# A fused attention and MLP kernel: one score product issued a step ahead, and a copy out of PSUM issued behind an exponential

## The chip, the cores and the metric

The kernel runs on one core of one Trainium2 chip. The metric is the time of one execution on the device in microseconds (us). Before the change it is 755.63 us, the median of three runs (755.60 to 755.68).

## What is computed

`x` has 2048 tokens of 512 channels. It is normalized, goes through an attention with 32 heads of 16 channels in which each token sees the 256 tokens up to itself, and through an MLP with 1792 hidden channels; the result is `x + s * silu(MLP)`.

```python
def _A_ref(x, wqkv, wo):          # H = 32, Dh = 16, W = 256
    q, k, v = qkv[0], qkv[1], qkv[2]
    scores = jnp.einsum("bhqd,bhkd->bhqk", q, k) * (Dh ** -0.5)
    mask = (idx[:, None] - idx[None, :] >= 0) & (idx[:, None] - idx[None, :] < W)
    p = _softmax(jnp.where(mask[None, None], scores, -1e9), axis=-1)
    o = jnp.einsum("bhqk,bhkd->bhqd", p, v)
    return o @ wo
...
def _B_ref(x, w1, b1, w2, b2):
    h = _gelu(_layernorm(x) @ w1 + b1)
    return h @ w2 + b2
...
xn = _layernorm(x)
s = _A_ref(xn, A_wqkv, A_wo)
g = _silu(_B_ref(xn, B_w1, B_b1, B_w2, B_b2))
return x + s * g
```

## The kernel before

Every engine runs its instructions in the order of the program text (`Ordered`); waits between engines are put in by the framework from the tiles that two instructions share. All matrix products are in single precision, split into a high and a low part where they are large.

**The attention loop.** The 32 heads are worked on four at a time (`n` = 0 to 7), in 16 blocks of 128 tokens, so there are 128 steps `t` = 16n + block. A first pass of 16 steps with negative `t` prepares the first heads. In step `t` TensorE (PE) issues, in this order:

1. `prob_block(..., 1)`: two products of keys and queries for two of the four heads into the PSUM tile `stb`. ScalarE (ACT) takes the exponential of it into a tile `pt` in SBUF, and GpSimd (POOL) zeroes what the mask excludes. There is one `stb`, so the next products into it wait for this exponential.
2. `max_block`, for the block `m = t + 12`, twelve steps ahead: four products into `xy` (the two newer key blocks), then, from the third block of a head on, four products into `zo[:, :, 0:256]` (the oldest key block, of which a triangle counts). VectorE (DVE) then copies that triangle from `zo` over the masked triangle of `xy` (`copy_predicated`), and reduces `xy` to its negated row maximum (`tensor_reduce`), which is later subtracted in the softmax. For the first two blocks of a head there is no oldest block, and the masked copy reads a constant instead of `zo`.
3. `fill_in(t, 0)`: a share of other matrix work, the "fills".
4. `prob_block(..., 0)`: the products and the exponential for the other two heads, through the same `stb`.
5. `fill_in(t, 1)`: more fills.
6. `pv_step`, for block `t - 1`: twelve products of probabilities and values (four for the first block of a head, eight for the second), in tiles of 128 rows by 17 columns, into `otb`. This is not a tile of its own but `zo[:, 1, 256:384]`. ACT then copies it into `oraw` in SBUF.

In what follows the exponential of 1 is called the **first** and that of 4 the **second** exponential of a step, and the stretch of a step that begins with each its first and second **half**. In the last twelve steps there is no block left for `max_block`, and the first products of a step go into `xy`.

**The fills.** The fills of the steps from 3 on are made by `tandem`: two jobs (`pair_qk`: projections of queries and keys for later heads; `pair_v`: of the values; `pair_h`: hidden products of the MLP) run through the two PSUM banks `fb[0]` and `fb[1]` at once. A unit is a pair of products of 64 rows each, one into each bank; two jobs of `pair_qk` are 24 units. When both jobs end, ACT copies bank 0 and DVE bank 1 (`closing`), and the next two jobs begin. `room(t, k)` says how many units half `k` of a step may take before others are preferred: mostly three in the first half and one in the second.

**After the loop** come the rest of the MLP, the output projection and the final sums, from about 435 us on, almost all of it a dense stream of products. The change does not touch that part.

Of the kernel before, what the change touches and what calls it, by code (L numbers as in the profile page):

```python
# [18 lines left out]
P = 128  # L19
NCH = S // 512  # L20
NKB = S // P
KT = D // P
# [27 lines left out]
def mixer_kernel(ctx, tc, x, wqk, wv, wo, w1, b1, w2, b2, out):  # L50


    nc = SimpleNamespace(**{name: Ordered(tc, name) for name in ("tensor", "vector", "scalar", "gpsimd", "sync")})
# [117 lines left out]
    slots = []  # L171
# [8 lines left out]
    oT_d = dram.tile([4, 8, 32, S], F32, name="oT_d")  # L180
# [8 lines left out]
    xy = psum.tile([P, 2, 512], F32, name="xy")  # L189
    zo = psum.tile([P, 2, 512], F32, name="zo")  # L190
    otb = zo[:, 1, 256:384]
    psf = attn.enter_context(tc.tile_pool(name="psf", bufs=1, space=PSUM))
    fb = [psf.tile([P, 512], F32, name=f"fb{i}") for i in range(2)]
# [103 lines left out]
    fills = {}  # L297
    closing = {}
# [145 lines left out]
    def tandem(t0, t1, one, two, mid=None, back=None):  # L444

        n = one[0]
        lo, hi = slice(0, 64), slice(64, P)
        mid = mid or max(1, (t0 + t1 + 1) // 2)  # L450
        late = t1 >= 16 * NQ - LEAD

        def room(t, k):

            m = t % 16
            if k:
                return {1: 3, 2: 2, 14: 2, 15: 2}.get(m, 1)
            return 2 if t == t0 else {4: 4, 15: 2}.get(m, 3)

        def places(slots, last):  # L460

            halves = [(t, k) for t in slots for k in (0, 1)] + [(t1, 0)] * last
            units = dict.fromkeys(halves, 0)
            for _ in range(n - last * n // 12):
                h = min(units, key=lambda h: (units[h] >= room(*h) * n // 12, units[h]))
                units[h] += 1
            if last:
                units[t1, 1] = n // 12
            return [h for h in units for _ in range(units[h])]

        def places_late(slots, last):

            last = min(n // 4, n // (len(slots) + 1)) if last else 0
            cuts = [(n - last) * k // len(slots) for k in range(len(slots) + 1)]
            out = []
            for t, a, b in zip(slots, cuts, cuts[1:]):
                ahead = min(b - a, max(n // 4, (b - a + 1) // 2))
                out += [(t, 0)] * ahead + [(t, 1)] * (b - a - ahead)
            return out + [(t1, 0)] * last

        deal = places_late if late else places
        first, second = deal(range(t0, mid), False), deal(range(back or mid, t1), True)
        for phase, where in enumerate((first, second)):
            for i in range(n):
                flags = dict(start=(phase == 0 and i == 0), stop=(phase == 1 and i == n - 1), skip_group_check=True)
                def unit(i=i, phase=phase, flags=flags):
                    (two if phase == 0 else one)[1](fb[1 - phase], i, hi, **flags)
                    (one if phase == 0 else two)[1](fb[phase], i, lo, **flags)
                fills.setdefault(where[i], []).append((unit, ()))
        closing[t1] = (one[2], (fb[0], t1, nc.scalar.copy)), (two[2], (fb[1], t1, nc.vector.tensor_copy))  # L490
        if late:
            fills[t1, 0].extend(closing.pop(t1))

    def spread(jobs, places):

        out, left = {}, list(places)
        for j, (ops, finish) in enumerate(jobs):
            n = round(len(left) / (len(jobs) - j))
            mine, left = left[:n], left[n:]
            for k, (_, mm, i) in enumerate(ops):  # L500
                out.setdefault(mine[k * n // len(ops)], []).append((mm, (i,)))
            out[mine[-1]].append((finish, ()))
        return out
# [1 line left out]

    mts = {}

    def max_block(n, qb):

        slot = slots[n % 2]  # L510
        if qb % 4 == 0:
            mts[n, qb // 4] = small.tile([P, 2, 2, 4], F32, tag="mt", name=f"mt_{n}_{qb}")
        lo = max(qb - 1, 0)
        off = 128 * (lo + 1 - qb)

        def scores(p, a, first):
            r = slice(64 * a, 64 * a + 64)
            out, keys = ((zo[:, a, P * p: P * (p + 1)], slice(P * (qb - 2), P * (qb - 1))) if first else
                         (xy[:, a, 256 * p + off: 256 * (p + 1)], slice(P * lo, P * (qb + 1))))
            nc.tensor.matmul(out, slot[r, 0, p, P * qb: P * (qb + 1)], slot[r, 1, p, keys], start=True, stop=True)  # L520

        for p, a, first in ((0, 1, False), (0, 0, False), (1, 1, False), (1, 0, False),
                            (0, 1, True), (0, 0, True), (1, 1, True), (1, 0, True)):
            if qb >= 2 or not first:
                scores(p, a, first)
        four = xy.rearrange("q a (p k) -> q a p k", p=2)
        nc.vector.copy_predicated(four[:, :, :, 128:256], mask,
                                  neg if qb < 2 else zo[:, :, 0:256].rearrange("q a (p k) -> q a p k", p=2))
        nc.vector.tensor_reduce(out=mts[n, qb // 4][:, :, :, qb % 4],
                                in_=four[:, :, :, off:256],  # L530
                                axis=AX.X, op=ALU.max, negate=True)
# [41 lines left out]
        pts[(n, kb, p)] = pt  # L573


    outs = {}

    def pv_step(n, qb):

        lo = max(qb - 2, 0)  # L580
        for kb in range(lo, qb + 1):
            for j in range(4):
                nc.tensor.matmul(otb[32 * j: 32 * j + DH + 1], vt[:, kb, (4 * n + j) % 16],
                                 pts[n, kb, j // 2][:, j % 2, P * (qb - kb): P * (qb - kb + 1)],
                                 start=(kb == lo), stop=(kb == qb),
                                 skip_group_check=True, tile_position=(0, 32 * j))
        if qb % 4 == 0:
            outs[0] = sgp.tile([P, 512], F32, tag="or", name=f"oraw_{n}_{qb}", bufs=2)
        nc.scalar.copy(outs[0][:, P * (qb % 4): P * (qb % 4 + 1)], otb)
        if qb % 4 == 3:  # L590
            (at if n or qb > 7 else behind)(16 * n + qb + 2, nc.sync.dma_start, oT_d[n // 2, n % 2::2, :, P * (qb - 3): P * (qb + 1)], outs[0])


    mlp = {}
# [151 lines left out]
        fills.setdefault(place, []).extend(todo)  # L746
    soon = {}
    tandem(3, 8, pair_qk(1, 2), pair_qk(1, 3))
    for n, spans in enumerate((((9, 14, 12), (15, 19, 18)), ((20, 24, 22), (25, 30, 28)), ((31, 35, 34), (36, 40, 38)),
                               ((41, 46, 44), (47, 51, 50)), ((74, 79, 77), (80, 84, 83)), ((85, 90, 88), (93, 98, 97))), 2):  # L750
        for c, span in zip((0, 2), spans):
            tandem(*span[:2], pair_qk(n, c), pair_qk(n, c + 1), *span[2:])
    for i, span in enumerate(((52, 56, 54), (57, 62, 60), (63, 67, 66), (68, 73, 71))):
        tandem(*span[:2], pair_v(2 * i), pair_v(2 * i + 1), *span[2:])
    for f, *span in ((6, 99, 104, 102), (8, 105, 110, 108), (10, 111, 115, 114), (12, 116, 121, 118, 119), (2, 122, 127, 124, 125)):
# [59 lines left out]
    def fill_in(t, half):  # L815
        now[:] = t, half
        run(delayed.pop((t, half), ()))
        for fn, args in fills.get((t, half), ()):
            fn(*args)

    end = 16 * NQ
    for t in range(-16, end + 1):
        m = t + LEAD
        if t == -5:
            open_slot(1)
            for k in range(4):
                at(-4 + k, clear_part, k)
        if 0 <= t < end:
            if t == 0:
                early.close()  # L830
                stb.append(attn.enter_context(tc.tile_pool(name="ps_s2", bufs=1, space=PSUM)).tile(
                    [P, 2, 512], F32, name="stb"))
            prob_block(t // 16, t % 16, 1)
        if t >= 0 and m < end:
            max_block(m // 16, m % 16)
        fill_in(t, 0)
        for fn, args in plan.get(t, []):
            fn(*args)
        if m == 1:
            max_block(0, 1)  # L840
        if 0 <= t < end:
            prob_block(t // 16, t % 16, 0)
        fill_in(t, 1)
        if m == 0 or 1 <= m < LEAD - 1:
            max_block(0, m + (m > 0))
        for fn, args in closing.get(t, ()):
            fn(*args)
        if t >= 1:
            pv_step((t - 1) // 16, (t - 1) % 16)
        run(lns.get(t, ()))  # L850
        done = m if t >= 0 else m + 1 if 0 < m < LEAD - 1 else 0
        if done < end and done % 4 == 3:
            max_rows(done // 16, done % 16 // 4, t)
        for fn, args in ends.get(t, []):
            fn(*args)
    for k in sorted(delayed):
        run(delayed[k])
    for fn, args in plan[end + 1]:
# [440 lines left out]
```

## Time and profile before

| | us |
|---|---|
| time, median of three runs | 755.63 |
| the profiled execution's own time | 756.44 |
| its span, first to last instruction | 754.6 |
| first exponential of step 0 | 64.79 |
| first exponential of step 112 | 391.97 |
| last first exponential (step 127) | 429.87 |

In a view of the timeline each row has a start and a length in us, the engine, the operation and what it writes and reads (`out<-in`); `x4` at the end is four instructions in one row, and brackets hold the idle time of that engine before the row and what ended it. PEld is the weight load of TensorE, which runs ahead of the products. All rows carry line L42, since a helper records every operation; they are told apart by their tiles. `zo<-qk` are the oldest-block products, `zo<-pt,vt` those of probabilities and values, `fb<-...` the fills.

### The profile page before, as it was taken

How to read it: one execution, taken by the hardware profiler on the slowest of the kernel's cores; microseconds unless marked ns; L12 is line 12 of the kernel's file. 1: busy time of each engine (PE TensorE's matmuls, PEld its weight loads, DVE VectorE, ACT ScalarE, POOL GpSimd, SP SyncE). 2: the span in 40 equal slices, each digit the busy share in tenths (PEclk: the TensorE clock that was granted, in tenths of full speed). 3: DMA queues.
4: the chain of work that ended last, by engine and by line, in shares of the span. 5: the costliest groups of instructions: out<-in, count | busy, mean ns of one | idle time of the engine just before them, and what ended most of it. 6: DMA issues, size and time to landing. Idle time of an engine off the chain costs nothing.

```text
span 754.6 us, 18785 instructions
## 1 busy us (share of the span) xinstructions
PE 742.7 (98%) x7412; PEld 581.8 (77%) x7412; DVE 502.6 (67%) x770; ACT 438.5 (58%) x745; POOL 313.4 (42%) x658
## 2 busy tenths in 40 slices
PE   8999999999999999999999999999999999999997
PEld 7886776777778887676676788888888888888886
DVE  7876676776767767787872547853666765676373
ACT  7747767767667676787877845444554643442001
POOL 7623767777566565877876700030102000001102
PEclk9999999999999999999999999999999999999999
DMA  8623355645347763546725383542112232244531
GB/s 285 192 62 83 74 146 135 172 114 123 90 105 217 256 212 98 147 108 183 202 77 158 91 296 103 167 158 66 57 42 97 85 111 71 69 158 136 172 93 56
DMA packets 56951, 99.40 MB, mean 132 GB/s; under 512 B 11104, under 2 KB 11360, under 8 KB 56864
## 3 DMA queue, kind: packets, MB, share of 16 engines
q1 hardware_dynamic: 56864, 98.21, 44.4%
q8 instruction: 58, 0.95, 0.5%
q14 instruction: 29, 0.24, 0.1%
HBM read 51.39 MB, written 29.62 MB: 107 GB/s over the span
## 4 chain that ended last, share of the span: by engine, by line
PE 88%; DVE 4%; ACT 2%; DMA 2%; POOL 2%; issue 1%; SPq 0%; DVEq 0%; ACTq 0%; POOLq 0%
PE acc L42 20%; PE fb L42 17%; PE zo L42 13%; PE p L42 9%; PE stb L42 8%; PE s L42 6%; PE h L42 6%; PE xy L42 5%; PE pv L42 3%; POOL pt L42 1%; ACT pt L42 1%; DVE mt L42 1%; DVE xnT L42 1%; DVE xy L42 1%; DMA oT_d<-oraw 1%
## 5 line engine op out<-in xcount | busy, mean ns | idle before, releaser
L42 POOL TENSOR_SCALAR_AFFINE_SELECT pt<-pt 128x256 f32<-128x256 f32 x480 | 188.2, 417 | 121.8 <-ACT pt L42 118.0
L42 ACT ACTIVATE pt<-stb 128x768 f32<-128x768 f32 (+1 forms) x244 | 188.4, 772 | 59.9 <-PE stb L42 50.9
L42 DVE TENSOR_REDUCE mt<-xy 128x4 f32<-128x1024 f32 (+1 forms) x128 | 152.6, 1192 | 4.4
L42 DVE COPY_PREDICATED xy<-upper,zo 128x512 f32<-128x512 int32 x112 | 77.9, 696 | 87.6 <-PE zo L42 84.4
L42 PE MATMUL acc<-w,gh 128*128 128x512 f32 x432 | 133.5, 390 | 0.0
L42 PE MATMUL fb<-xnT,wqb 64*128 64x512 f32 (+1 forms) x684 | 116.3, 405 | 0.3 <-DVE xnT L42 0.2
L42 POOL TENSOR_TENSOR xo<-xo,gated 128x512 f32<-128x512 f32 x15 | 20.2, 1348 | 216.9 <-DVE gated L42 212.6
L42 PE MATMUL zo<-pt,vt 128*17 128x128 f32 x2880 | 103.8, 275 | 0.3 <-POOL pt L42 0.3
L42 PE MATMUL stb<-qk 64*128 64x384 f32 (+1 forms) x488 | 97.7, 396 | 2.5 <-ACT pt L42 0.8
L42 PEld LDWEIGHTS zo<-pt,vt 128*17 128x17 f32 x2880 | 67.6, 97 | 37.6 <-DVE xy L42 19.8
L42 PEld LDWEIGHTS acc<-w,gh 128*128 128x128 f32 x432 | 80.8, 188 | 16.6
L42 PE MATMUL acc<-w,gl 128*128 128x512 f32 x216 | 84.4, 391 | 0.0
L42 PEld LDWEIGHTS stb<-qk 64*128 64x128 f32 x488 | 45.7, 183 | 48.3 <-ACT pt L42 37.3
L42 PEld LDWEIGHTS fb<-xnT,wqb 64*128 64x128 f32 (+1 forms) x684 | 63.9, 187 | 7.0 <-issue 0.6
L42 PE MATMUL xy<-qk 64*128 64x256 f32 (+2 forms) x536 | 61.3, 302 | 1.4 <-DVE mt L42 1.0
L42 ACT COPY oraw<-zo 128x128 f32<-128x128 f32 x128 | 34.3, 268 | 37.4 <-PE zo L42 27.1
L42 PEld LDWEIGHTS xy<-qk 64*128 64x128 f32 x536 | 43.1, 185 | 11.2 <-DVE mt L42 4.5
L42 PEld LDWEIGHTS acc<-w,gl 128*128 128x128 f32 x216 | 40.6, 188 | 8.9 <-DVE gl L42 0.7
L42 ACT ACTIVATE gated<-acc 128x512 f32<-128x512 f32 x16 | 8.7, 595 | 65.2 <-DVE acc L42 65.2
L42 PE MATMUL s<-wos,ohl 128*128 128x512 f32 (+1 forms) x204 | 44.7, 378 | 0.0
L42 PEld LDWEIGHTS s<-wos,ohl 128*128 128x128 f32 x204 | 36.7, 188 | 6.9
L42 ACT COPY p<-p 128x512 f32<-128x512 f32 x21 | 12.3, 585 | 49.8 <-PE p L42 42.3
(198 smaller groups left out, 1196.5 us busy)
## 6 DMA issues: line engine op xcount, KB each, us to landing
qk<-sh SPq DMA_DIRECT2D x128, 128.0 KB
qk<-pjr SPq DMA_DIRECT2D x64, 128.0 KB
oT_d<-oraw SPq DMA_DIRECT2D x32, 256.0 KB
w_d<-in_w_dram SPq DMA_DIRECT2D x14, 512.0 KB
x<-in_x_dram SPq DMA_DIRECT2D x16, 256.0 KB
or<-oT_d SPq DMA_DIRECT2D x16, 256.0 KB
w<-rden_d SPq DMA_DIRECT2D x16, 256.0 KB
xo<-in_x_dram SPq DMA_DIRECT2D x16, 256.0 KB
```

The costliest lines, as they stand in the source:

```text
L42: r = issue(*args, **kwargs)
```

## The change

**Oldest-block products ahead.** `first_scores` holds the four products into `zo` that `max_block` had. They are now issued in the step before: behind `fill_in(t, 1)` and ahead of `pv_step`, for block `m + 1`. Blocks without an oldest block are left out, and three early ones keep their old place.

**The copy of the values.** `pv_step` no longer issues ACT's copy of `otb`. It leaves a function in the list `copies`, which is called in the next step, behind the first exponential and ahead of `max_block`.

**The fills.** `room` now gives four units to the first half and mostly none to the second. The eight window pairs of heads 2 to 5 (steps 9 to 51) go through the new `staggered`: the job in bank 1 starts four units behind that in bank 0 and ends four units into the next pair; both banks are copied by DVE, one step apart. The first four units at step 9 and the last four at step 51 are single products.

```diff
@@ room of tandem, and how halves are dealt
             m = t % 16
             if k:
-                return {1: 3, 2: 2, 14: 2, 15: 2}.get(m, 1)
-            return 2 if t == t0 else {4: 4, 15: 2}.get(m, 3)
+                return {1: 2, 2: 1, 3: 1, 4: 1}.get(m, 0)
+            return 3 if t == t0 else {5: 3, 15: 3}.get(m, 4)
...
+    AHEAD = 4
+    def staggered(windows):
...
+        for w, (t0, t1, mid, one, two) in enumerate(windows):
+            head = [(t0, 0)] * AHEAD
+            laid.append((head + deal(range(t0 + 1, mid), n - AHEAD, None, mid - 1), deal(range(mid, t1), n, t1)))
...
+            for i in range(n):
+                if i >= AHEAD:
+                    unit(first[i], two[1], 1, i - AHEAD, hi, i == AHEAD, False)
+                elif w:
+                    unit(first[i], windows[w - 1][4][1], 1, n - AHEAD + i, hi, False, i == AHEAD - 1)
+                unit(first[i], one[1], 0, i, lo, i == 0, False)
...
+            closing[t1] += ((one[2], (fb[0], t1, nc.vector.tensor_copy)),)
...
+            closing[t1 + 1] += ((two[2], (fb[1], t1, nc.vector.tensor_copy)),)
...
+    def first_scores(n, qb):
+        slot = slots[n % 2]
+        keys = slice(P * (qb - 2), P * (qb - 1))
+        for p in range(2):
+            for a in (1, 0):
+                r = slice(64 * a, 64 * a + 64)
+                nc.tensor.matmul(zo[:, a, P * p: P * (p + 1)], slot[r, 0, p, P * qb: P * (qb + 1)],
+                                 slot[r, 1, p, keys], start=True, stop=True)
...
+        if qb >= 2 and not ahead:
+            first_scores(n, qb)
         four = xy.rearrange("q a (p k) -> q a p k", p=2)
         nc.vector.copy_predicated(four[:, :, :, 128:256], mask,
                                   neg if qb < 2 else zo[:, :, 0:256].rearrange("q a (p k) -> q a p k", p=2))
...
-        nc.scalar.copy(outs[0][:, P * (qb % 4): P * (qb % 4 + 1)], otb)
+        out = outs[0]
+        def copy_out():
+            nc.scalar.copy(out[:, P * (qb % 4): P * (qb % 4 + 1)], otb)
+        copies.append(copy_out)
...
             prob_block(t // 16, t % 16, 1)
+        while copies:
+            copies.pop()()
         if t >= 0 and m < end:
-            max_block(m // 16, m % 16)
+            max_block(m // 16, m % 16, m in early_first)
...
         fill_in(t, 1)
+        if t >= 0 and m + 1 < end and (m + 1) % 16 >= 2 and ((m + 1) % 4 or m >= 32):
+            first_scores((m + 1) // 16, (m + 1) % 16)
+            early_first.add(m + 1)
```

**ACT, steps 42 to 44.** `pt_10`, `pt_11` and `pt_12` are the exponentials of these steps, `_1` the first and `_0` the second; `oraw<-zo` is the copy of the values. In brackets stand the engines on whose counts of finished instructions the row waits. Before:

```order
L42 ACTIVATE pt_10_0_2960<-stb 128x768 [waits PE_49]
L42 COPY oraw_8_2934<-zo 128x128 [waits DVE_49,PE_49]
L42 ACTIVATE pt_11_1_2982<-stb 128x768 [waits PE_49,Activation_49,Pool_49]
L42 ACTIVATE pt_11_0_3004<-stb 128x768 [waits PE_49]
L42 COPY oraw_8_2934<-zo 128x128 [waits DVE_49,PE_49]
L42 ACTIVATE pt_12_1_3029<-stb 128x768 [waits PE_49,Activation_49,Pool_49]
```

and now:

```order
L42 ACTIVATE pt_10_0_2966<-stb 128x768 [waits PE_49]
L42 ACTIVATE pt_11_1_2989<-stb 128x768 [waits PE_49,Activation_49,Pool_49]
L42 COPY oraw_8_2934<-zo 128x128 [waits DVE_49]
L42 ACTIVATE pt_11_0_3010<-stb 128x768 [waits PE_49]
L42 ACTIVATE pt_12_1_3036<-stb 128x768 [waits PE_49,Activation_49,Pool_49]
```

The copy moved from between the second exponential of one step and the first of the next to behind that first one.

**PE, second half of step 43.** `stb` are the products for the second exponential, `zo<-qk` the oldest-block products, `zo<-pt` those of probabilities and values. Before:

```order
L42 MATMUL stb<-qk_92 128x384 [waits Activation_49]
L42 MATMUL stb<-qk_92 128x384
L42 MATMUL fb_108<-xnT,wqb_2804 128x512
L42 MATMUL fb_109<-xnT,wqb_2804 128x512
L42 MATMUL zo<-pt_9_0_2912,vt 17x128 [waits DVE_49]
L42 MATMUL zo<-pt_9_0_2912,vt 17x128
L42 MATMUL zo<-pt_9_1_2889,vt 17x128 x2
L42 MATMUL zo<-pt_10_0_2960,vt 17x128 x2
L42 MATMUL zo<-pt_10_1_2938,vt 17x128 x2
L42 MATMUL zo<-pt_11_0_3004,vt 17x128 [waits Pool_49]
```

and now:

```order
L42 MATMUL stb<-qk_92 128x384 [waits Activation_49]
L42 MATMUL stb<-qk_92 128x384
L42 MATMUL zo<-qk_722 128x128 [waits DVE_49]
L42 MATMUL zo<-qk_722 128x128 x3
L42 MATMUL zo<-pt_9_0_2909,vt 17x128 x2
L42 MATMUL zo<-pt_9_1_2885,vt 17x128 x2
L42 MATMUL zo<-pt_10_0_2966,vt 17x128 x2
L42 MATMUL zo<-pt_10_1_2937,vt 17x128 x2
L42 MATMUL zo<-pt_11_0_3010,vt 17x128 [waits Pool_49]
```

The unit of fills went to the first half, the oldest-block products came in its place, and the wait on DVE now stands ahead of them.

**DVE, steps 67 to 69, now.** `COPY_PREDICATED` is the masked copy of `max_block`, reading `zo` in the first row and the constant `negc` in the fourth (the first block of a head). Both kinds of row read alike before the change:

```order
L42 COPY_PREDICATED xy<-upper,zo 128x4x128 [waits DVE_49,PE_49,Activation_49]
L42 TENSOR_REDUCE mt_12_4109<-xy 128x4 [waits DVE_49]
L42 COPY vt<-fb_109 128x32x16 [waits PE_49]
L42 COPY_PREDICATED xy<-upper,negc 128x4x128 [waits DVE_49,PE_49]
L42 TENSOR_REDUCE mt_0_4342<-xy 128x4 [waits DVE_49]
L42 STREAM_TRANSPOSE mT_3_4333<-mh_3_4330 128x32 [waits DMAHW1_49,Pool_49]
```

DVE's order of these rows did not move. A masked copy that reads `zo` waits for ACT, one that reads the constant does not. In the built program the ACT count that it waits for is, before and now, the one that the latest copy of the values reaches. That copy stood ahead of the first exponential of the step and now stands behind it.

## What is predicted, and from which rows

> **What bounds the kernel now.** I read the page first, then the view of waits, then one ordinary step in the timeline.
>
> ```profile
> span 754.6 us, 18785 instructions
> PE 742.7 (98%) x7412; PEld 581.8 (77%) x7412; DVE 502.6 (67%) x770; ACT 438.5 (58%) x745; POOL 313.4 (42%) x658
> ```
>
> ```profile
> DVE xy L42 <- PE zo L42: 84.4, 95, 1.9
> ACT pt L42 <- PE stb L42: 50.9, 121, 0.9
> PEld stb L42 <- ACT pt L42: 37.3, 147, 1.0
> ```
>
> PE is busy for 98% of the span, but in the attention loop that is not the whole story: PE's weight loads wait for ACT's exponentials (37.3 us over 147 waits) and ACT for PE's products (50.9 us), because there is one `stb`. The largest wait, 84.4 us of the masked copy for the oldest-block products, is on DVE, which has time to spare. Step 43, an ordinary one, shows the turn:
>
> ```profile
> 190.33 0.19 PEld L42 LDWEIGHTS stb<-qk 64*128 64x128 f32 x2 [0.21 <-ACT pt L42]
> ...
> 190.61 0.41 PE L42 MATMUL xy<-qk 64*128 64x256 f32 x4
> 190.79 0.30 PEld L42 LDWEIGHTS zo<-qk 64*128 64x128 f32 x4
> 190.86 0.37 PE L42 MATMUL zo<-qk 64*128 64x128 f32 x4
> 190.90 0.81 ACT L42 ACTIVATE pt<-stb 128x768 f32<-128x768 f32 x1 [0.16 <-PE stb L42]
> 191.00 0.53 PEld L42 LDWEIGHTS fb<-xnT,wqb 64*128 64x128 f32 x6
> ...
> 191.33 0.70 DVE L42 COPY_PREDICATED xy<-upper,zo 128x512 f32<-128x512 int32 x1 [0.86 <-PE zo L42]
> 191.76 0.18 PEld L42 LDWEIGHTS stb<-qk 64*128 64x128 f32 x2 [0.22 <-ACT pt L42]
> ...
> 192.04 0.40 PE L42 MATMUL fb<-xnT,wqb 64*128 64x512 f32 x2
> 192.06 1.23 DVE L42 TENSOR_REDUCE mt<-xy 128x4 f32<-128x1024 f32 x1
> ...
> 192.24 0.81 ACT L42 ACTIVATE pt<-stb 128x768 f32<-128x768 f32 x1 [0.53 <-PE stb L42]
> 192.36 0.57 PEld L42 LDWEIGHTS zo<-pt,vt 128*17 128x17 f32 x24 [0.31 <-DVE xy L42]
> ...
> 193.14 0.19 PEld L42 LDWEIGHTS stb<-qk 64*128 64x128 f32 x2 [0.21 <-ACT pt L42]
> ...
> 193.28 0.27 ACT L42 COPY oraw<-zo 128x128 f32<-128x128 f32 x1 [0.23 <-DVE mt L42]
> ...
> 193.71 0.81 ACT L42 ACTIVATE pt<-stb 128x768 f32<-128x768 f32 x1 [0.17 <-PE stb L42]
> 194.42 0.61 ACT L42 CAST sh<-pjr 128x512 fp32r<-128x512 f32 x1
> ```
>
> From first exponential to first exponential the step takes 193.71 − 190.90 = 2.81. The first half is 192.24 − 190.90 = 1.34, and `stb` is all of it: exponential .81, .05 until PE loads weights (191.71 to 191.76), .48 until the next exponential (191.76 to 192.24). The second half is 193.71 − 192.24 = 1.47; there PE's stream of products is the limit. The copy of the values (.27) lies in a gap of ACT and costs nothing.
>
> **The change: a new ring of waits.** The step of the sum that decides is the masked copy on DVE. Its rows in the order above say that it waits for ACT, and the count is that of the latest copy of the values, since `otb` is part of the tile `zo` that both read. Before, that copy ended before the first exponential (193.28 + .27 = 193.55, against 193.71), while the masked copy starts .43 behind its own (191.33 against 190.90), so the wait cost nothing. Now the copy stands behind the first exponential. Nothing else would hold the masked copy, since its `zo` was filled a step earlier; so it waits for the copy. Behind it on DVE wait its own reduction, the closings and the transposes. On PE the oldest-block products for the next block wait for it, since they overwrite the `zo` it reads; the products of values stand behind these, and behind those the products for the next first exponential. So the ring closes, once a step, from the weight load for the first `stb` to the next:
>
> - load for `stb` to the first exponential, 190.33 to 190.90: .57
> - exponential to the start of ACT's next operation, 193.71 to 194.42: .71
> - the copy of the values: .27
> - ACT's end to the masked copy's start: no row. PE picks up behind ACT in .05 (191.71 to 191.76), DVE behind PE in .10 (190.86 + .37 = 191.23 to 191.33). I take .05, the one with the same releaser; .10 stays for the range.
> - masked copy: .70, and .05 more until PE's load for `zo` (as PE behind ACT)
> - load for the oldest-block products to the load for the products of values. No row has the one behind the other; the products take 191.23 − 190.79 = .44, and in the row before the loads of values start at 192.36, .08 ahead of the end of the last fill (192.04 + .40). So .36. If the loads could follow as those of a fill do, it would be .21 (190.79 to 191.00); I take .36, since these have the tiles of the products of values.
> - load of values to the next load for `stb`, 192.36 to 193.14: .78
>
> The sum is **3.49**, against 2.81: +.68 for an ordinary step.
>
> At the last handover a page bears on it. The trace has products of 64 rows by 128 ahead of loads of 128 by 17. The Trainium skill, "TensorEngine Tiling (Array Packing)", section "Key Properties", says that a change of tiling mode drains TensorE. By that rule the loads stay behind nearly all of the products, which is what 192.36 against 192.44 shows, and the sum stays; without it the step would be 3.34, the third rival below.
>
> **The sixteen steps of a head group.** Not all are ordinary. The rows that tell the others:
>
> ```profile
> 162.43 0.13 PEld L42 LDWEIGHTS zo<-pt,vt 128*17 128x17 f32 x8 [0.37 <-POOL pt L42]
> ...
> 165.87 0.35 PEld L42 LDWEIGHTS zo<-pt,vt 128*17 128x17 f32 x16 [0.36 <-issue]
> ...
> 200.59 0.60 ACT L42 ACTIVATE pt<-stb 128x512 f32<-128x512 f32 x1 [0.69 <-PE stb L42]
> ...
> 201.95 0.38 ACT L42 ACTIVATE pt<-stb 128x256 f32<-128x256 f32 x1
> ```
>
> - Step 1 (four products of values, 8 loads): .57 − .13 = .44 less, 3.05. Step 2 (16 loads): .22 less, 3.27.
> - Step 3 has no oldest-block products ahead: .36 less, 3.13.
> - Steps 4 and 5: the masked copy reads the constant and does not wait for ACT. No ring; they stay at 2.81 each.
> - Steps 14 and 15 have shorter exponentials: .81 − .60 = .21 and .81 − .38 = .43 less, 3.28 and 3.06.
> - The other nine are ordinary, 31.41.
>
> That is 31.41 + 3.05 + 3.27 + 3.13 + 5.62 + 3.28 + 3.06 = 52.8. Before, 112 steps took 391.97 − 64.79 = 327.18, or 46.74 for sixteen:
>
> ```profile
> 64.79 0.80 ACT L42 ACTIVATE pt<-stb 128x768 f32<-128x768 f32 x1
> ...
> 391.97 0.81 ACT L42 ACTIVATE pt<-stb 128x768 f32<-128x768 f32 x1 [0.16 <-PE stb L42]
> ...
> 404.10 0.81 ACT L42 ACTIVATE pt<-xy 128x768 f32<-128x768 f32 x1 [0.27 <-DVE hr L42]
> ...
> 409.93 0.81 ACT L42 ACTIVATE pt<-xy 128x768 f32<-128x768 f32 x1 [0.16 <-PE xy L42]
> ...
> 411.48 0.84 ACT L42 ACTIVATE pt<-xy 128x768 f32<-128x768 f32 x1
> ...
> 429.87 0.38 ACT L42 ACTIVATE pt<-xy 128x256 f32<-128x256 f32 x1
> ```
>
> - Seven head groups: 7 x 6.08 = **+42.6**.
> - Three first halves (steps 10, 26, 42) take eight units of fills, some 1.8 of products; most of it fits between the first exponential and the oldest-block products, and I add .2 each, an estimate: **+.6**.
> - Steps 8, 12 and 16 keep the oldest-block products in their old place. There these wait for the copy, and the masked copy for them, .54 later (190.79 to 191.33); the steps ahead of them save .36. 3 x .18 = **+.5**.
> - Steps 112 to 115: 3.49 + 3.05 + 3.27 + 3.13 = 12.9 against 404.10 − 391.97 = 12.1: **+.8**.
> - From 116 on there is no masked copy, but the products of values overwrite `otb` and wait for the copy themselves: .57 + .71 + .27 + .05 + .78 = 2.38 a step. Of the eleven steps between 404.10 and 429.87 five are shorter, the shortest 411.48 − 409.93 = 1.55. Raising them to 2.38 gives .83 for that one and 1.3 for the other four: **+2.1**.
>
> The sum is +46.6. The profiled execution took 756.44 (span 754.6 and 1.84 around it), so 803.0. It lies .81 above the median of the runs (755.63); on the median that is **802**.
>
> **What I cost at nothing.** Per ordinary step PE now has .68 of slack, and so:
>
> - Fills in the first half: the PE work of a step is the same, only moved to where PE waits for the ring anyway. Uncovered, a unit moved into a half that PE fills costs .225 (rival one).
> - The staggered windows' eight single units: a unit of two products is about .20 (192.04 + .40 for a pair, less overlap); 8 x .20 = 1.6 at most, in two steps with slack.
> - Closings moved from ACT to DVE: .68 each; DVE then has .70 + 1.23 + .68 = 2.61 in such a step, under 3.49. The next unit may wait for the bank within the first half; uncovered that is up to .3 at sixteen places, 5 us.
> - ACT's casts (.61) behind the copy instead of ahead of it, and SP's sends that follow them: ACT has .81 x 2 + .27 + .61 = 2.50 in such a step, under 3.49. Uncovered, .25 at a second exponential (.71 + .27 + .61 = 1.59 against the first half's 1.34).
>
> **The rivals.**
>
> *One: the masked copy is not held, and the kernel is a little faster.* The place is the masked copy of an ordinary step, and it decides by when the copy of the values has ended: if before the products into `xy` end (190.61 + .41 = 191.02 in step 43, .12 behind the first exponential's start), the ring never forms. By the rows the copy would end .98 behind it (.71 + .27), .86 too late; only a wait met by another count could spare it. Then the step gains what was meant:
>
> ```profile
> 170.06 0.81 ACT L42 ACTIVATE pt<-stb 128x768 f32<-128x768 f32 x1
> ...
> 171.41 0.81 ACT L42 ACTIVATE pt<-stb 128x768 f32<-128x768 f32 x1
> ...
> 173.33 0.81 ACT L42 ACTIVATE pt<-stb 128x768 f32<-128x768 f32 x1
> ```
>
> Step 36 has three units in its second half, 1.92 against 1.47 with one: .225 a unit. Seven such steps lose two units there: −3. Three first halves take four units more: +2.7. Some 75 ordinary second halves can fall from 1.47 towards the first half's 1.34; I take a third of that, −3. The time would be about 755.6 − 3.3 = 752. For it speaks only that the two readers of `zo` touch different columns. The Trainium skill, "PSUM — Partial Sum Buffer", section "PSUM bank collisions raise a hardware error", has the rule that PSUM is guarded by bank and quadrant, not by address, and that this holds for two readers on ACT and DVE; by it the wait stands and the sum stays. No run here shows a collision.
>
> *Two: a dearer ring.* The copy may not overlap the exponential's end: .81 instead of .71, some 100 times, +10; the masked copy may start .10 behind it, +5. About 812 to 817.
>
> *Three: a cheaper ring.* The loads of values follow the oldest-block products after .21 instead of .36, in some 89 steps: −13, 789.
>
> *Four: DVE as the bound,* with its closings. Against it stands 2.61 under 3.49; it would add the 5 us named above, 807, inside the range.
>
> **How the numbers follow.** The ring as summed, with its small errors and the fourth rival: .66. The dearer ring .14, the cheaper one .14, no ring .06. The range leaves the no-ring case out and takes in the bounds of both unknown handovers: 788 to 818. Faster by over 0.2% (about what a measurement of this kernel can tell from no change) is the no-ring case less a third of it that ends within 0.2%: .04. Within 0.2% .02, slower .94.
>
> **What would show it.** In the changed profile an ordinary step should take about 3.5 from first exponential to first exponential; the copy of the values should start .7 behind that exponential; the masked copy should name ACT and `oraw` as its releaser and start within .1 of the copy's end; and the oldest-block products should name DVE. Two steps of sixteen should keep 2.8. ACT and PE together should wait some 45 us longer in the loop, and what lies behind 435 us should only be shifted. If the masked copy starts right behind the products into `xy`, rival one holds and the sum falls with it.

## The result and the profile after

The changed kernel takes **804.68 us** (median of four runs, 804.11 to 805.54) against 755.62 before (755.40 to 755.68): the ratio is 1.065, with a 95% interval of 1.0633 to 1.0667. The profiled execution has a span of 803.8 us, 49.2 more than before.

The head of the page of the changed kernel:

```profile
span 803.8 us, 18686 instructions
PE 760.8 (95%) x7412; PEld 592.1 (74%) x7412; DVE 506.4 (63%) x778; ACT 420.5 (52%) x737; POOL 314.4 (39%) x658
```

Every engine has about the instructions that it had (eight closings went from ACT to DVE), and a smaller share of the span. PE's busy time grew by 18.1 us for the same 7412 products, and ACT's fell by 18.0; neither makes 49.2 us. What grew are the waits of the engines for each other. The view of waits of the changed kernel (us in total, number, longest) says where:

```profile
ACT pt L42 <- PE stb L42: 149.8, 183, 2.3
DVE xy L42 <- ACT oraw L42: 114.2, 96, 2.1
PEld zo L42 <- DVE xy L42: 50.1, 88, 0.7
PE zo L42 <- DVE xy L42: 24.9, 64, 0.5
PEld stb L42 <- ACT pt L42: 24.8, 89, 1.0
DVE xy L42 <- PE zo L42: 13.4, 11, 1.9
```

Before, the masked copy (`xy` on DVE) waited for the oldest-block products, 95 times. That wait is gone but for 11 times, and another stands in its place, 96 times: the masked copy waits for ACT's copy of the values (`oraw`). Read the next rows as a chain: PE's oldest-block products wait for the masked copy, and ACT's exponentials wait for PE three times as long as before (149.8 us against 50.9).

Step 43 in the timeline of the changed kernel, the same step as before the change:

```profile
208.96 0.19 PEld L42 LDWEIGHTS stb<-qk 64*128 64x128 f32 x2 [0.23 <-ACT pt L42]
...
209.52 0.81 ACT L42 ACTIVATE pt<-stb 128x768 f32<-128x768 f32 x1 [0.62 <-PE stb L42]
210.23 0.26 ACT L42 COPY oraw<-zo 128x128 f32<-128x128 f32 x1
210.39 0.18 PEld L42 LDWEIGHTS stb<-qk 64*128 64x128 f32 x2 [0.26 <-ACT pt L42]
...
210.52 0.69 DVE L42 COPY_PREDICATED xy<-upper,zo 128x512 f32<-128x512 int32 x1 [1.94 <-ACT oraw L42]
...
211.27 0.30 PEld L42 LDWEIGHTS zo<-qk 64*128 64x128 f32 x4 [0.70 <-DVE xy L42]
...
211.64 0.57 PEld L42 LDWEIGHTS zo<-pt,vt 128*17 128x17 f32 x24
...
212.42 0.19 PEld L42 LDWEIGHTS stb<-qk 64*128 64x128 f32 x2 [0.21 <-issue]
...
212.99 0.81 ACT L42 ACTIVATE pt<-stb 128x768 f32<-128x768 f32 x1 [1.30 <-PE stb L42]
```

Going down the rows, each waits for the one before it: exponential, copy of the values .71 behind its start, masked copy .03 behind the copy's end, oldest-block products .06 behind the masked copy's end, products of values .37 behind the start of those, products for the next exponential. (The load at 210.39, for the second exponential, is not part of this chain.) From 208.96 to 212.42 the ring takes 3.46; the step takes 212.99 − 209.52 = 3.47. The largest idle times of the step, 1.94 of DVE and 1.30 of ACT, lie on it.

### The profile page after: what moved, and what is told of

It is laid out like the page before. It is cut to its first block, busy times and chain, and to the rows that moved or that the text cites. A ratio compares the mean times of both kernels' runs of the same rounds, so it can differ in the third digit from the quotient of the medians.

```text
span 803.8 us, 18686 instructions
## 1 busy us (share of the span) xinstructions
PE 760.8 (95%) x7412; PEld 592.1 (74%) x7412; DVE 506.4 (63%) x778; ACT 420.5 (52%) x737; POOL 314.4 (39%) x658
## 4 chain that ended last, share of the span: by engine, by line
PE 47%; ACT 2%; DVE 2%; DMA 1%; issue 1%; SPq 0%; ACTq 0%; DVEq 0%
PE acc L42 19%; PE p L42 8%; PE s L42 5%; PE h L42 5%; PE zo L42 4%; PE fb L42 2%; ACT pt L42 2%; DVE xy L42 1%; PE stb L42 1%; DMA w<-w_d 1%; PE yt L42 1%; PE xy L42 1%; ACT oraw L42 0%; DMA xnT<-w_d 0%; DVE hr L42 0%
## 5 line engine op out<-in xcount | busy, mean ns | idle before, releaser
L42 ACT ACTIVATE pt<-stb 128x768 f32<-128x768 f32 (+1 forms) x244 | 188.9, 774 | 158.0 <-PE stb L42 149.8
L42 DVE COPY_PREDICATED xy<-upper,zo 128x512 f32<-128x512 int32 x112 | 77.9, 696 | 131.9 <-ACT oraw L42 114.2
L42 PE MATMUL fb<-xnT,wqb 64*128 64x512 f32 (+1 forms) x684 | 109.7, 402 | 1.3 <-DVE xnT L42 0.6
L42 PE MATMUL stb<-qk 64*128 64x384 f32 (+1 forms) x488 | 100.6, 401 | 1.3 <-ACT pt L42 0.7
L42 PEld LDWEIGHTS fb<-xnT,wqb 64*128 64x128 f32 (+1 forms) x684 | 66.6, 187 | 14.1 <-DVE pjr L42 3.5
L42 PE MATMUL zo<-qk 64*128 64x128 f32 x448 | 46.1, 284 | 25.9 <-DVE xy L42 23.0
L42 PEld LDWEIGHTS zo<-qk 64*128 64x128 f32 x448 | 34.4, 186 | 48.7 <-DVE xy L42 44.6
L42 PE MATMUL xy<-qk 64*128 64x256 f32 (+2 forms) x536 | 59.6, 296 | 2.4 <-DVE mt L42 1.4
L42 PEld LDWEIGHTS xy<-qk 64*128 64x128 f32 x536 | 45.5, 184 | 12.3 <-DVE mt L42 7.2
```

Of the source, the lines that this page charges most:

```text
L42: r = issue(*args, **kwargs)
```

## The experiments

Most of the experiments tell the ring apart from two rivals: that the oldest-block products ahead of the products of values cost the time by themselves, and that the new fills do. The others ask what the products ahead, the fills and the windows are worth once the ring is gone. Each diff stands against the kernel named.

**The copy put back.** Against the changed kernel:

```diff
-        copies.append(copy_out)
+        copy_out()
...
-    copies.pop()()
```

> The changed kernel with one thing undone: ScalarE's copy of the values stands right behind the products of values again, ahead of the next first exponential. Oldest-block products ahead and the new fills stay. Ring theory (the masked copy waits for the copy of the values, which waits for the first exponential): the copy ends before the exponential begins, the masked copy starts about .8 us behind the load for stb instead of 1.6, ordinary steps fall from 3.46 to 2.75 to 2.85, the time to 748 to 757 us. Rival (the oldest-block products ahead of the products of values cost the time by themselves, by the switch of tiles or by standing in front of them): the steps stay above 3.2 and the time above 790. Rival (the fills moved to the first half and the staggered windows cost it): the time stays above 790 too.

Measured: 754.33 us (ratio to before .9988, .9976 to 1.0000). One copy of .27 us a step, in its old place, takes back the whole loss; whether this kernel is faster than the one before the change is not clear of the interval. An ordinary step in the timeline of this kernel:

```profile
180.21 0.18 PEld L42 LDWEIGHTS stb<-qk 64*128 64x128 f32 x2 [0.23 <-ACT pt L42]
...
180.33 0.27 ACT L42 COPY oraw<-zo 128x128 f32<-128x128 f32 x1 [0.17 <-PE zo L42]
...
180.78 0.82 ACT L42 ACTIVATE pt<-stb 128x768 f32<-128x768 f32 x1 [0.18 <-PE stb L42]
180.99 0.70 DVE L42 COPY_PREDICATED xy<-upper,zo 128x512 f32<-128x512 int32 x1 [0.82 <-PE xy L42]
...
181.65 0.19 PEld L42 LDWEIGHTS stb<-qk 64*128 64x128 f32 x2 [0.25 <-ACT pt L42]
...
181.75 0.36 PEld L42 LDWEIGHTS zo<-qk 64*128 64x128 f32 x4
...
182.14 0.81 ACT L42 ACTIVATE pt<-stb 128x768 f32<-128x768 f32 x1
182.19 0.57 PEld L42 LDWEIGHTS zo<-pt,vt 128*17 128x17 f32 x24
...
183.00 0.19 PEld L42 LDWEIGHTS stb<-qk 64*128 64x128 f32 x2 [0.24 <-ACT pt L42]
...
183.56 0.81 ACT L42 ACTIVATE pt<-stb 128x768 f32<-128x768 f32 x1 [0.19 <-PE stb L42]
```

The copy of the values is done at 180.60, before the exponential begins; the masked copy starts as soon as `xy` is ready, .78 behind the load for `stb`, and neither the oldest-block products nor those of values wait for anything. The step takes 183.56 − 180.78 = 2.78, against 2.81 before the change. What is late now is visible too: both loads for `stb` wait for an exponential (.25 and .24). The step is bound by the two exponentials through the one `stb`, and the products ahead and the new fills together gain .03 of it. The masked copy's long wait has not gone either; it is now for the products into `xy` instead of those into `zo`:

```profile
DVE xy L42 <- PE xy L42: 77.3, 95, 2.3
DVE xy L42 <- PE zo L42: 13.0, 12, 1.9
```

**Only the copy moved.** Against the kernel before:

```diff
-    outs = {}
+    outs, copies = {}, []
...
-        nc.scalar.copy(outs[0][:, P * (qb % 4): P * (qb % 4 + 1)], otb)
+        out = outs[0]
...
+        def copy_out():
+            nc.scalar.copy(out[:, P * (qb % 4): P * (qb % 4 + 1)], otb)
...
+        copies.append(copy_out)
...
+        while copies:
+            copies.pop()()
         if t >= 0 and m < end:
             max_block(m // 16, m % 16)
...
+    copies.pop()()
```

> The kernel before with one thing changed: the copy of the values goes behind the next first exponential. Oldest-block products and fills are as before. Ring theory: now the oldest-block products, in their old place behind xy, wait for the copy, and the masked copy for them: .57 + .71 + .26 + .05 + .54 + .70 + .05 + .78 = 3.66 for an ordinary step, and the fills and the second stb stand behind the waiting products as well, so rather 3.7 to 3.9; the time 825 to 850 us, slower than the whole change. Rivals (oldest-block products ahead, or the fills, cost the time): the copy lies in a gap of ScalarE, so 755 to 762 us.

Measured: 853.33 us in one run, 3 us above the range. The move of one copy alone costs twice what the whole change does. From its timeline:

```profile
224.26 0.81 ACT L42 ACTIVATE pt<-stb 128x768 f32<-128x768 f32 x1 [0.65 <-PE stb L42]
224.97 0.26 ACT L42 COPY oraw<-zo 128x128 f32<-128x128 f32 x1
225.28 0.30 PEld L42 LDWEIGHTS zo<-qk 64*128 64x128 f32 x4 [1.04 <-ACT oraw L42]
...
228.15 0.81 ACT L42 ACTIVATE pt<-stb 128x768 f32<-128x768 f32 x1 [0.65 <-PE stb L42]
```

PE itself now waits for the copy, 1.04 us, and the fills and the second `stb` products stand behind the waiting weights. The step takes 3.89, the upper end of what was expected. In the changed kernel the products ahead soften this, as its step of 3.47 shows: they move PE's wait to the second half, behind the second `stb`.

**The copy twice.** Against the changed kernel:

```diff
-            nc.scalar.copy(out[:, P * (qb % 4): P * (qb % 4 + 1)], otb)
+            for _ in range(2):
+                nc.scalar.copy(out[:, P * (qb % 4): P * (qb % 4 + 1)], otb)
```

> The changed kernel with the copy of the values issued twice in a row (the same bytes). Ring theory: each step whose ring holds the copy is longer by one copy, .22 to .27 us; there are 14 of 16 such steps in the 116 and all of the last twelve, some 113, so +25 to +31: 830 to 836 us. Rivals: ScalarE is busy for 52% of the span and the copy off the path, so within 3 us of 804.7.

Measured: 836.15 us in one run, +31.5, just above the top of the range. (Steps 8 and 12 took 5.80 and 5.87 there, for a reason told in the last section; ordinary steps took 3.74.) The waits of the masked copy for `oraw` rose from 114.2 to 143.5 us:

```profile
DVE xy L42 <- ACT oraw L42: 143.5, 97, 3.2
```

An instruction of .26 us on an engine that is busy for half of the span is paid in full, once a step: 3.74 against 3.47. So the copy lies on the ring.

**The copy behind the masked copy.** Against the changed kernel:

```diff
-        while copies:
-            copies.pop()()
         if t >= 0 and m < end:
             max_block(m // 16, m % 16, m in early_first)
+        while copies:
+            copies.pop()()
```

> The changed kernel with the copy of the values issued behind max_block instead of ahead of it, still behind the first exponential. The masked copy then no longer waits for it; the copy waits for the masked copy, and the oldest-block products ahead wait for the copy. Ring theory: masked copy from .79 to 1.49 behind the load for stb, copy to 1.81, load of the oldest-block products 1.86, + .37 + .78 = 3.0 for an ordinary step instead of 3.46, about 5.6 us less in sixteen steps and 39 in all: 760 to 770 us. If the place of the copy behind the exponential costs by itself, and not the masked copy's wait: about 800.

Measured: 771.76 us in one run, 33 less than the changed kernel. Its timeline in an ordinary step:

```profile
195.26 0.19 PEld L42 LDWEIGHTS stb<-qk 64*128 64x128 f32 x2 [0.23 <-ACT pt L42]
...
196.03 0.70 DVE L42 COPY_PREDICATED xy<-upper,zo 128x512 f32<-128x512 int32 x1 [1.64 <-PE xy L42]
...
196.76 0.27 ACT L42 COPY oraw<-zo 128x128 f32<-128x128 f32 x1
...
197.08 0.30 PEld L42 LDWEIGHTS zo<-qk 64*128 64x128 f32 x4 [0.20 <-ACT oraw L42]
...
198.23 0.19 PEld L42 LDWEIGHTS stb<-qk 64*128 64x128 f32 x2 [0.21 <-ACT pt L42]
```

The same copy on the same engine, still behind the first exponential: only the order of the two readers of `zo` is turned round. The ring is now masked copy, copy, products, 2.97 in this step as expected, though many ordinary steps take 3.05 to 3.06, and the time is 2 us above the range. So two thirds of the loss come from the masked copy's wait. The rest, 771.76 − 754.33 = 17.4, stays with the copy behind the exponential: PE's loads now wait for the copy itself, as the row at 197.08 shows.

**The fills alone.** Against the changed kernel, copy put back and no products ahead:

```diff
-        copies.append(copy_out)
+        copy_out()
...
-        if t >= 0 and m + 1 < end and (m + 1) % 16 >= 2 and ((m + 1) % 4 or m >= 32):
-            first_scores((m + 1) // 16, (m + 1) % 16)
-            early_first.add(m + 1)
...
-    copies.pop()()
```

> Neither the oldest-block products ahead nor the copy behind the exponential: both stand where they stood before. Only the fills are new (four units in the first half, mostly none in the second, staggered windows). Ring theory, and that the step is bound by the exponentials through the one stb once the ring is gone (2.78 in the run with the copy put back): the second half's unit goes to .2 us of idle time in the first half, products of values start earlier, ordinary steps 2.77 to 2.80, the time 752 to 757 us, like the run with the copy put back: the products ahead then bring nothing. If the products ahead were what makes 2.78: steps of 2.85 and more, 758 to 765.

Measured: 760.54 us (ratio 1.0060, 1.0043 to 1.0077). The time expected, 752 to 757, was missed; what came is the other case that the expectation names, in which the products ahead are what makes 2.78. The timeline shows it:

```profile
182.76 0.19 PEld L42 LDWEIGHTS stb<-qk 64*128 64x128 f32 x2 [0.41 <-ACT pt L42]
...
183.40 0.80 PEld L42 LDWEIGHTS fb<-xnT,wqb 64*128 64x128 f32 x8
...
184.21 0.23 PEld L42 LDWEIGHTS stb<-qk 64*128 64x128 f32 x2
...
185.71 0.19 PEld L42 LDWEIGHTS stb<-qk 64*128 64x128 f32 x2 [0.40 <-ACT pt L42]
```

With the oldest-block products still in the first half, the fourth unit does not fit: the second load for `stb` follows the fills without waiting for ACT (184.21), while PE waits .40 in the second half. The step takes 185.71 − 182.76 = 2.95. I had taken the .22 that PE waited in the first half before for room, and a unit of fills takes about that. But the second exponential here starts at 184.85, .64 behind its load, where it started .48 behind before the change: the fills still stand in front of the `stb` products. So with these fills the products ahead are worth about 760.5 − 754.3 = 6 us: they make the room that the fourth unit needs. Against the kernel before, the two together gain next to nothing.

**No staggered windows, copy put back.** Against the run with the copy put back:

```diff
-            if n < 6:
-                staggers.append((t0, t1, mid, pair_qk(n, c), pair_qk(n, c + 1)))
-            else:
-                tandem(t0, t1, pair_qk(n, c), pair_qk(n, c + 1), mid)
-    staggered(staggers)
+            tandem(t0, t1, pair_qk(n, c), pair_qk(n, c + 1), mid)
```

> The changed kernel with the copy of the values put back, and with the eight staggered windows run by tandem in the same spans (both banks begin and end together). It tells what the staggering is worth where no ring hides it: each window then waits for both banks at its start, up to .3 us, and saves eight single units, 1.6 us: 753 to 758 us against 754.3. If staggering costs, it is below 753.

Measured: 752.81 us (ratio .9956, .9941 to .9971), below the range and 1.5 below the same kernel with staggered windows. No kernel here is clearly faster. The staggering saves nothing that this run could find. How much it costs stays open: the two spans differ by 752.2 − 750.5 = 1.7, of which .7 lies in the first 112 steps, and the rest ahead of the first step and behind the last, where the two programs are alike.

**No staggered windows, ring left.** The same edit on the changed kernel itself.

> The changed kernel with the eight staggered windows run by tandem in the same spans; copy behind the exponential and products ahead stay. Ring theory: the fills lie in time in which TensorE waits anyway, so ordinary steps stay 3.46 and the time 800 to 807 us. If the staggered windows carry part of the loss: below 790.

Measured: 805.36 us in one run, against 804.68 with them. The windows carry nothing of the loss.

**The copy on VectorE.** Against the changed kernel:

```diff
-            nc.scalar.copy(out[:, P * (qb % 4): P * (qb % 4 + 1)], otb)
+            nc.vector.tensor_copy(out[:, P * (qb % 4): P * (qb % 4 + 1)], otb)
...
-        copies.append(copy_out)
+        copy_out()
...
-    copies.pop()()
```

> The changed kernel with the copy of the values done by VectorE right behind the products of values, instead of ScalarE behind the exponential. Ring theory: no wait for an exponential is left in front of the masked copy, so ordinary steps 2.75 to 2.80 and 752 to 757 us; VectorE then has .70 + 1.23 + .68 + about .2 = 2.8 us of work in a step with a closing, which may add up to 2 us. If only the place on ScalarE behind the exponential mattered in another way (the products ahead, the fills): above 790.

Measured: 754.92 us (ratio .9983, .9973 to .9992). Taking .27 us a step off ACT brings nothing over the copy put back (754.33): there it lay in a gap ahead of the exponential.

**Three windows shifted.** Against the run without staggered windows, copy put back:

```diff
-    for n, spans in enumerate((((9, 13, 11), (14, 18, 17)), ((19, 24, 22), (25, 29, 27)), ((30, 34, 33), (35, 40, 38)),
-                               ((41, 45, 43), (46, 50, 49)), ((74, 79, 77), (80, 84, 83)), ((85, 90, 88), (93, 98, 97))), 2):
+    for n, spans in enumerate((((9, 13, 12), (14, 18, 17)), ((19, 24, 22), (25, 29, 28)), ((30, 34, 33), (35, 40, 38)),
+                               ((41, 45, 44), (46, 50, 49)), ((74, 79, 77), (80, 84, 83)), ((85, 90, 88), (93, 98, 97))), 2):
```

> The fastest kernel so far (products ahead, copy put back, no staggered windows: 752.8 us), and in the windows of steps 9, 25 and 41 the point at which the two jobs swap banks one step later. There step 9, 25 and 41 took 3.66 to 3.9 us, with four units in the second half. Ring theory and TensorE as the bound: these three steps fall to about 2.9, and steps 12, 28 and 44 take three units more in the second half, + .6 each: 1 us less in all, 751 to 753 us. If a unit in the second half costs nothing or is hidden: up to 2.5 us less.

Measured: 752.84 us (ratio .9964, .9952 to .9976), the same as without the shift. The load moved as expected (steps 9, 25 and 41 fell to 2.96 to 2.99, steps 12, 28 and 44 rose to 3.45 to 3.75) and so did the time that it takes: the first three lost 2.3 us together, the others gained 2.0. The 1 us that was expected in all is not there. A unit costs about as much wherever it goes, which fits a PE that is busy for 98% of this kernel.

## Why the prediction was right

The forecast was 802, the median 804.68 and 805.54 the profiled execution; the mechanism was the one forecast, and rival one (the masked copy not held) did not occur. By its steps:

**The ring.** Measured in step 43, against the terms of the sum: load for `stb` to exponential .56 (.57), exponential to copy .71 (.71), copy .26 (.27), to the masked copy .03 (.05), masked copy and PE's load behind it .75 (.75), oldest-block products to products of values 211.64 − 211.27 = .37 (.36), products of values to the next load .78 (.78). Sum 3.46 against 3.49. The two handovers without a row were the ones that the range was kept for: with .71 and .03 the ring is not dearer, and with .37 it is not cheaper. Nor is DVE the bound of an ordinary step (rival four): it idles for 1.94 ahead of the masked copy. The .37 also agrees with the rule of the Trainium skill, "TensorEngine Tiling (Array Packing)", section "Key Properties", on the change of tiling mode: the loads in tiles of 128 by 17 stay behind nearly all of the .44 that the 64-row products take, where the loads of a fill follow after .21.

**The stages.** These rows of the changed kernel mark them (first exponentials of steps 0, 112, 116 and 127):

```profile
64.49 0.80 ACT L42 ACTIVATE pt<-stb 128x768 f32<-128x768 f32 x1
...
437.91 0.81 ACT L42 ACTIVATE pt<-stb 128x768 f32<-128x768 f32 x1 [1.34 <-PE stb L42]
...
451.53 0.81 ACT L42 ACTIVATE pt<-xy 128x768 f32<-128x768 f32 x1 [0.98 <-DVE hr L42]
...
479.31 0.38 ACT L42 ACTIVATE pt<-xy 128x256 f32<-128x256 f32 x1 [0.98 <-PE xy L42]
```

| stage | predicted | measured |
|---|---|---|
| steps 0 to 112 | +43.7 (42.6 + .6 + .5) | (437.91 − 64.49) − 327.18 = +46.2 |
| steps 112 to 116 | +.8 | (451.53 − 437.91) − 12.13 = +1.5 |
| steps 116 to 127 | +2.1 | (479.31 − 451.53) − 25.77 = +2.0 |
| ahead of step 0 and behind step 127 | 0 | −.5 |
| sum | +46.6 | +49.2 |

**What was mis-sized.** The sum came within 2.6 partly because errors cancel. Two terms were too small by 4.7 together. Step 4 of each head group, taken at 2.81 because its masked copy waits for no copy, took 3.25 in the mean of seven (2.81 to 4.13), +3.1 in all. Part of this was there before: the same seven steps took 3.07 in the mean before the change, which an ordinary step of 2.81 does not show. And step 52, the longest with 4.13, took 4.03 with the copy put back, so it is not the ring that makes it long. What the ring can add shows in step 68, where the cover that I named for the closings is missing, since no ring is there to hide them:

```profile
292.55 0.68 DVE L42 COPY vt<-fb 128x512 f32<-128x512 f32 x1
292.68 0.30 PEld L42 LDWEIGHTS xy<-qk 64*128 64x128 f32 x4 [0.30 <-DVE mt L42]
...
293.28 0.77 PEld L42 LDWEIGHTS fb<-wva,xnT 64*128 64x128 f32 x12 [0.30 <-DVE vt L42]
...
293.98 0.19 PEld L42 LDWEIGHTS stb<-qk 64*128 64x128 f32 x2
```

The closing on DVE (`vt`) comes late, since the masked copy and the reduction of step 67 were late; the next fills wait for their bank, and the second `stb` products stand behind them. The other is step 8, one of the three early ones: 94.97 − 89.37 = 5.60 instead of 3.49 + .54 = 4.03, for a reason told below; steps 12 and 16, with 4.08 and 4.09, are as summed. Against these, 45 ordinary steps of 3.46 instead of 3.49 give back 1.2, and step 14 of each group, with 3.14 instead of 3.28, gives back 1.0. One reading of the sum was wrong without harm: from step 116 on, six steps were below 2.38 before, not five, and the term is 2.2 instead of 2.1. The .7 by which steps 112 to 116 were missed lies in the last two of them, 3.52 and 3.63 instead of 3.27 and 3.13; why was not followed.

**What was costed at nothing.** That it costs nothing is shown for the staggered windows (805.36 without them, 804.68 with them). For the closings it did not hold in step 68. For the fills in the first half with the ring left, for the casts and for SP's sends it was not tried by itself.

## What to carry to other kernels

When an instruction is moved behind another, list who waits for *it*, not only what it waits for: here a copy of .27 us that cost nothing became 49 us, because two readers of one PSUM tile wait for each other in program order, and the second of them holds the engine that feeds the first. Where two uses share a tile, the order of their readers is a dependency that no line of the kernel shows; look for it in the waits of the built order, and put the reader that others wait for first. And before a long wait is removed, see what is late next: with the copy put back, the masked copy's 84.4 us of wait for `zo` fell to 13.0, but 77.3 us of wait for `xy` stood in its place, and an ordinary step was only .03 us shorter, since the exponentials through the one `stb` bound it.

## What was not expected of the hardware

The clock of TensorE fell in kernels whose ring lets it wait for about 1 us at a time at most. In the windows of the changed kernel (us, busy time of PE, PEld, DVE, ACT, POOL, granted clock, DMA share, GB/s):

```profile
87.00:90.40 3.40, 2.32 (x38) 1.25 (x34) 1.92 (x2) 2.44 (x6) 3.16 (x8) 1.00 0.09 34
90.40:94.40 4.00, 4.00 (x42) 3.17 (x42) 2.73 (x4) 1.29 (x2) 1.41 (x4) 0.57 0.01 1
94.40:97.00 2.60, 2.15 (x20) 1.54 (x16) 1.00 (x2) 2.03 (x4) 1.15 (x3) 1.00 0.03 4
```

PE was busy for 68% of the 3.4 us ahead, with .81 as the longest wait for weights in step 8 and .70 just before; then the granted clock was .57 over 4 us, and there six fill products took 1.60 where six took .91 in step 43 before the change. Most of step 8's 1.6 us lies here: without staggered windows and with the ring left, the clock held in step 8, and it took 4.06. By the mean clock it does not happen every time: of the four runs of the changed kernel, two have a mean clock of 1.000 and took 804.11 and 804.21, and two have .998 and .996 and took 805.54 and 805.16. A fall was seen once, elsewhere, in the run without staggered windows with the ring left, and twice in the run with the copy twice; in none of the runs without the ring, nor in the one with only the copy moved, though PE was busy for just 76% of the time in many stretches there (3.05 of 4 us). The Trainium skill, "TensorE: Matmul & The Clock Gate", section "What's actually happening", puts a fall to half clock behind at least one idle window of about 3.4 us; here no idle time of PE near that length stands ahead of the fall in the trace, so a window that is idle in part has been enough. But PE's busy share alone does not decide. In this same kernel PE was busy for 2.34 us between 103.2 and 106.6 and the clock stayed full, and in the run with the copy on VectorE, where PE waits 2.12 us for a transfer, it was busy for just 38%:

```profile
253.90:257.30 3.40, 1.28 (x22) 1.21 (x20) 1.06 (x3) 1.08 (x2) 1.88 (x3) 1.00 0.95 345
257.30:260.70 3.40, 3.40 (x64) 3.12 (x61) 2.39 (x4) 1.79 (x3) 1.53 (x4) 1.00 0.42 98
```

The clock was full there and in the 3.4 us behind. What decides stays open.
